# Attention and two expert layers on one core: v's row sums and a weight-conversion step placed on GpSimd

## The chip, the cores and the metric

The kernel runs on one core of a Trainium2 chip. The core has five engines with instruction streams of their own: TensorE (PE in the profile, with its weight loads as PEld), VectorE (DVE), ScalarE (ACT), GpSimd (POOL) and SyncE (SP), which here only issues DMAs. Each engine runs its stream in order and waits on semaphores for the others. The metric is the device time of one execution in microseconds, the median of the runs that were timed; lower is better.

## The reference

Inputs are q, k and v (4 batches, 8 heads, 576 positions, 64 features), and two pairs of weights, `w_in` 512 x 2048 and `w_out` 2048 x 512, all drawn as 64-bit floats. What has to be computed, cut to its core:

```python
q_d = q.reshape(B, H, Sd, 4, D).mean(axis=3)     # the same for k_d, v_d; Sd = 144
out_d = softmax(q_d @ k_d.T / 8) @ v_d           # whole rows
out_up = np.repeat(out_d, 4, axis=2)
mask = np.abs(pos[:, None] - pos[None, :]) < 4
out_local = softmax(where(mask, q @ k.T / 8, -1e9)) @ v
x = (out_up + out_local)  ->  2304 tokens x 512
h = x @ w1_in;   g = h * sigmoid(1.702 * h);  y = g @ w1_out
h = y @ w2_in;   g = elu(h);                  out = g @ w2_out
```

`mean` of four rows of v is the sum that this change is about; the kernel adds four rows and puts the factor 0.25 on the result of the product.

## The kernel before

The attention is done in units. A unit is one pair of heads of one batch: four `early` units (batch 0, windows 0 to 3) and four `late` units (batch 0, windows 4 to 8, which take the downsampled part from their early unit), then twelve units of `rest` (batches 1 to 3). `whole` is the list early + rest, the sixteen units that have a downsampled part. The two layers follow, each as products in float32r with a high and a low part of both operands: `products_h1` (L766) and `products_y1` (L801) for layer 1, `products_h2` (L914) and `products_o2` (L963) for layer 2. The first two token blocks of layer 1 (256 tokens each) run while the attention of batches 1 to 3 is still going on, and while the weights are still being converted.

**Weights.** A weight tile (128 x 512 numbers of 64 bits, `wst`) is loaded as integers and turned into a high and a low float32r part by `conv_w`. L158 takes the high words of the 64-bit numbers, read at every second word, times 2^-112 and writes `ww`; three buffers of `ww` exist. L165 (DVE) shifts in place, L168 (ACT, first 20 tiles of layer 1; for the others DVE) sets the sign bits in place, L171 (DVE) joins `ww` and the low words, L178 (ACT) makes the high part `whl`, L182 (DVE) the low part. There are 32 tiles in layer 1 (`i0, i1, o0, o1, i2, ...`; i is w_in, o is w_out) and 32 in layer 2. L158 is on ScalarE for both layers. L136 and L141 load the tiles from SP's queue.

**Rows of v.** For the product `pvd` (L582) a unit needs `vd`, where each row is the sum of four rows of v. The early units do this with `add_vd`: one load per head (`vr`, L389, from SP), and three additions on POOL (L394, L396). All units of `rest` do it with `load_vd`: row 0 by a load from SP (L378), rows 1 to 3 by DMAs from POOL's queue that add into the destination (L380), six per unit. `pv_down` of a unit starts this for the unit four places later in `whole`; `vd` has four buffers.

**Room.** Early units 1 to 3 have no room of their own for most tiles; `LENT` and `spare` give them parts of the buffers of layer-1 weights that are loaded late (o15, i15, o14, ... down to o8), and the next one, i8, holds `ones`, the operand of the filler products `keep_busy` (L853), which keep TensorE occupied at the start.

**Order.** In the start phase the code order fixes PE's stream, with two fillers after each piece of attention; elsewhere a scheduler orders the instructions of each engine by its own estimates of durations. No engine's order follows from the code alone, so the change moves instructions also on engines that it doesn't name.

Of the kernel before, what the change touches and what calls it, by code (L numbers as in the profile page):

```python
# [8 lines left out]
F32 = mybir.dt.float32  # L9
# [6 lines left out]
AF = mybir.ActivationFunctionType  # L16
ALU = mybir.AluOpType
# [3 lines left out]
D = 64  # L21
S = 576
SD = 144
HALF = 72
# [11 lines left out]
FIRST = 4  # L36

LENT = {
    "rawq": (0, "rawq", 0), "pd": (0, "pd", 0),
    "rawk": (1, "rawk", 0), "pdT": (1, "pdT", 0),  # L40
# [26 lines left out]
def kernel(  # L67
# [20 lines left out]
    nc = tc.nc  # L88
    B, H = q.shape[0], q.shape[1]
    NHP = H // 2  # L90
# [16 lines left out]
    for half in range(2):  # L107
        rows = slice(64 * half, 64 * half + 64)
        for a, e, lo in ((0, 1, -3), (1, 5, 0), (5, 6, 3)):
            m = mask[rows, a:e, :]  # L110
            for step, base, mult in ((1, -lo, -1), (-1, lo + 6, 1)):
                nc.gpsimd.affine_select(
                    out=m, in_=m, pattern=[[0, e - a], [step, KW]], compare_op=ALU.is_ge, fill=NEG,
# [30 lines left out]
    def conv_w(pool, bufs, layer, kind, f, sign):  # L144
# [8 lines left out]
        low, high = words[:, :, 0], words[:, :, 1]  # L153
        halves = t.bitcast(U16).rearrange("p (n four) -> p n four", four=4)
        w = pool.tile([P, NK * P], F32, tag="ww", name=f"ww{layer}{kind}{f}", bufs=bufs)
        wi = w.bitcast(I32)
        w3 = w.rearrange("p (c n) -> p c n", c=NK)
        nc.scalar.activation(out=w, in_=high.bitcast(F32), func=AF.Copy, scale=2.0 ** -112)  # L158

        def middle():  # L160
            shifts = [(0, 1, ALU.logical_shift_right, 13)]
# [145 lines left out]
    class Unit:  # L307
# [38 lines left out]
        def load_qk(self):  # L346
# [14 lines left out]
            for nm, src in (("q", q), ("k", k)):  # L361
# [5 lines left out]
                        out=r[:, :, j, :], in_=src[b, 2 * hp + j].rearrange("(p t) d -> p t d", t=6)  # L367
                    )
                self.raw.append(r)
        def load_vd(self):  # L370

            b, hp = self.b, self.hp
            self.vd = self.t([HALF, 2, 2, D], "vd", bufs=4)
            for r in range(4):
                for j in range(2):
                    src = v[b, 2 * hp + j].rearrange("(c g r) d -> g c r d", g=HALF, r=4)[:, :, r, :]
                    if r == 0:
                        nc.sync.dma_start(out=self.vd[:, :, j, :], in_=src)  # L378
                    else:
                        nc.gpsimd.dma_start(out=self.vd[:, :, j, :], in_=src, accum_op=ALU.add)  # L380

        def add_vd(self):

            b, hp = self.b, self.hp
            self.vd = self.t([HALF, 2, 2, D], "vd", bufs=4)
            for j in range(2):
                tag = ("gh", "gl", "gh", "g")[self.hp] if j == 0 else ("gh", "gl", "gl", "g")[self.hp]
                r = gpool.tile([HALF, 2, 4, D], F32, tag=tag, name=f"vr{j}_{self.n}", bufs=2 if tag == "g" else None)
                nc.sync.dma_start(  # L389
                    out=r.rearrange("g c r d -> g c (r d)"),  # L390
                    in_=v[b, 2 * hp + j].rearrange("(c g r) d -> g c (r d)", g=HALF, r=4),
                )
                vd = self.vd[:, :, j, :]
                nc.gpsimd.tensor_tensor(out=vd, in0=r[:, :, 0, :], in1=r[:, :, 1, :], op=ALU.add)  # L394
                for i in (2, 3):
                    nc.gpsimd.tensor_tensor(out=vd, in0=vd, in1=r[:, :, i, :], op=ALU.add)  # L396
# [181 lines left out]
        def pv_down(self):  # L578
            ps = self.ps([P, SD], "pvd")
            for kc in range(2):  # L580
                for j in range(2):
                    nc.tensor.matmul(  # L582
                        out=ps[64 * j:64 * j + 64, :], lhsT=self.vd[:, kc, j, :],
                        rhs=self.pdT[:, 2 * j + kc, :], start=(kc == 0), stop=(kc == 1),
                    )
            self.dn = self.t([P, SD], "dn", bufs=NHP)
            nc.scalar.activation(out=self.dn, in_=ps, func=AF.Copy, scale=0.25)
            at = whole.index(self) + 4
            if at < len(whole):
                whole[at].load_vd()  # L590

        def pv(self, w0, w1):
            dn = self.dn if self.dn_from is None else self.dn_from.dn
# [82 lines left out]
    whole = early + rest  # L676

    spare = [(kd, f) for f in range(NF - 1, 0, -1) for kd in "oi"]
    for part in (3, 4, 0, 1, 2):
        for u in early[1:]:  # L680
            u.lent[part] = spare.pop(0)
    following = dict(zip(units, units[1:]))
# [422 lines left out]
```

## Time and profile before

| what | value |
|---|---|
| median of 3 timed runs | 988.99 us (988.82 to 990.99) |
| span of the profiled execution | 1196.4 us, 15208 instructions |
| PE busy | 1183.7 us, 99% of the span |
| DVE, ACT, POOL busy | 503.3, 471.7, 102.0 us |
| granted TensorE clock, mean of the span | 0.750 |

The profiled execution is known by its span alone, and that is 207 us longer than the median of the timed runs. Shares and waits hold for the profiled execution; the timed ones had to be quicker somewhere. A granted clock of 1 is 2.4 GHz, a half is 1.2 GHz. Busy times are unions of an engine's instructions in a stretch, and a PE that is called busy is a model of its ends.

### The profile page before, as it was taken

What the parts mean: (1) busy time and instruction counts of PE and PEld (TensorE: products, weight loads), DVE (VectorE), ACT (ScalarE), POOL (GpSimd) and SP (SyncE); (2) the same over time, 40 slices, a digit from 0 to 9 for tenths busy, and PEclk for the clock granted to TensorE, in tenths of its full rate; (3) what the DMA queues carried; (4) which work ended last, traced back from release to release, by engine and by line L of the source; (5) the groups of instructions that cost most, each with busy time, mean ns of one, the idle gap of its engine ahead of it and who ended that gap; (6) DMA issues with size and microseconds to landing.
All of it is one profiled execution on the core that took longest, in us unless ns stands there. A gap on an engine that the chain in (4) does not pass through costs nothing.

```text
span 1196.4 us, 15208 instructions
## 1 busy us (share of the span) xinstructions
PE 1183.7 (99%) x6028; PEld 881.7 (74%) x6028; DVE 503.3 (42%) x898; ACT 471.7 (39%) x1116; POOL 102.0 (9%) x117
## 2 busy tenths in 40 slices
PE   9999999999999999999999999999999999999998
PEld 4578999976667677777668986677767777676787
DVE  3777785344453442122122796673213222221222
ACT  5888654233332441122113464553223222322233
POOL 4243210211230000000000000000000000000000
PEclk8777777776777777777777777777777777777777
DMA  9668612332331102100004940001001000100000
GB/s 194 157 157 225 145 27 39 68 58 34 47 52 23 43 16 74 44 3 33 1 1 128 315 156 0 1 14 58 1 1 35 27 1 1 44 0 1 1 36 18
DMA packets 128822, 68.04 MB, mean 57 GB/s; under 512 B 99184, under 2 KB 118768, under 8 KB 128752
## 3 DMA queue, kind: packets, MB, share of 16 engines
q1 hardware_dynamic: 109040, 63.21, 18.9%
q0 software_dynamic: 14976, 2.69, 2.7%
q10 hardware_dynamic: 4736, 1.18, 0.6%
q8 instruction: 47, 0.77, 0.3%
q14 instruction: 23, 0.19, 0.1%
HBM read 57.59 MB, written 9.44 MB: 56 GB/s over the span
## 4 chain that ended last, share of the span: by engine, by line
PE 97%; ACT 2%; DVE 1%; issue 0%; DVEq 0%; ACTq 0%
PE h L766 22%; PE y L801 21%; PE o L963 21%; PE h L914 20%; PE busy L853 3%; PE qk L468 2%; PE pv L598 2%; PE ptr L572 2%; PE qkd L495 1%; PE pvd L582 1%; PE pdt L560 1%; PE pt L421 1%; ACT pd L525 0%; DVE wst1i L165 0%; ACT sl L518 0%
## 5 line engine op out<-in xcount | busy, mean ns | idle before, releaser
L801 PE MATMUL y<-g1h,whl1o 128*128 128x256 f32 (+1 forms) x768 | 253.3, 401 | 0.0
L963 PE MATMUL o<-whl2o,g2h 128*128 128x512 f32 x576 | 214.1, 457 | 0.0
L766 PE MATMUL h<-xh,whl1i 128*128 128x256 f32 (+1 forms) x768 | 209.6, 406 | 0.3 <-ACT xh L299 0.3
L914 PE MATMUL h<-x2h,whl2i 128*128 128x512 f32 (+1 forms) x640 | 190.9, 427 | 0.0
L801 PEld LDWEIGHTS y<-g1h,whl1o 128*128 128x128 f32 x768 | 154.6, 217 | 35.6 <-issue 3.4
L766 PEld LDWEIGHTS h<-xh,whl1i 128*128 128x128 f32 x768 | 143.1, 219 | 35.2 <-issue 3.0
L924 DVE SCALAR_TENSOR_TENSOR g<-e,h 128x512 f32<-128x512 f32 (+1 forms) x80 | 50.7, 634 | 262.8 <-ACT e L922 262.6
L914 PEld LDWEIGHTS h<-x2h,whl2i 128*128 128x128 f32 x640 | 122.9, 201 | 45.6
L801 PE MATMUL y<-g1l,whl1o 128*128 128x256 f32 (+1 forms) x384 | 152.5, 397 | 0.0
L963 PEld LDWEIGHTS o<-whl2o,g2h 128*128 128x128 f32 x576 | 113.7, 199 | 46.5
L921 ACT ACTIVATE e<-h 128x512 f32<-128x512 f32 (+1 forms) x80 | 44.5, 556 | 252.2 <-PE h L914 252.2
L963 PE MATMUL o<-whl2o,g2l 128*128 128x512 f32 x288 | 131.7, 457 | 0.0
L776 ACT ACTIVATE g<-h 128x512 f32<-128x512 f32 x72 | 42.8, 596 | 202.2 <-PE h L766 200.6
L779 DVE SCALAR_TENSOR_TENSOR g<-g,h 128x512 f32<-128x512 f32 x72 | 49.1, 685 | 174.4 <-ACT g L776 174.4
L766 PE MATMUL h<-xl,whl1i 128*128 128x256 f32 (+1 forms) x384 | 107.5, 403 | 0.0
L380 POOL DMA_DIRECT2D vd<-in_v_dram x72 | 84.7, 1238 | 243.0 <-DMA vd<-in_v_dram 181.0
L914 PE MATMUL h<-x2l,whl2i 128*128 128x512 f32 (+1 forms) x320 | 95.7, 427 | 0.0
L801 PEld LDWEIGHTS y<-g1l,whl1o 128*128 128x128 f32 x384 | 83.8, 218 | 15.1 <-issue 0.3
L766 PEld LDWEIGHTS h<-xl,whl1i 128*128 128x128 f32 x384 | 72.9, 224 | 15.4 <-issue 2.0
L914 PEld LDWEIGHTS h<-x2l,whl2i 128*128 128x128 f32 x320 | 61.1, 201 | 21.7
L963 PEld LDWEIGHTS o<-whl2o,g2l 128*128 128x128 f32 x288 | 57.6, 200 | 23.9
L931 DVE TENSOR_TENSOR g2l<-g,g2h 128x512 fp32r<-128x512 f32 (+1 forms) x80 | 51.6, 645 | 36.7 <-ACT g2h L929 36.2
(110 smaller groups left out, 1185.6 us busy)
## 6 DMA issues: line engine op xcount, KB each, us to landing
wst1i<-in_moe_w_in_dram SPq DMA_DIRECT2D x16, 512.0 KB
wst1o<-in_moe_w_out_dram SPq DMA_DIRECT2D x16, 512.0 KB
wst2i<-in_moe_w_in_dram SPq DMA_DIRECT2D x16, 512.0 KB
wst2o<-in_moe_w_out_dram SPq DMA_DIRECT2D x16, 512.0 KB
ydram<-ye SPq DMA_DIRECT2D x18, 256.0 KB
out_dram<-ot SPq DMA_DIRECT2D x18, 256.0 KB
y<-ydram SPq DMA_DIRECT2D x16, 256.0 KB
vw<-in_v_dram SPq DMA_DIRECT2D x24, 122.5 KB
```

What stands on the lines that cost most here:

```text
L380: nc.gpsimd.dma_start(out=self.vd[:, :, j, :], in_=src, accum_op=ALU.add)
L468: nc.tensor.matmul(out=ps[r, w - a, :], lhsT=self.qkT[0][r, 64 * w:64 * w + 64], rhs=self.qkT[1][r, ks:ks + KW], start=not by_pe, stop=Tru ...
L766: nc.tensor.matmul(out=ph[:, i, :], lhsT=w_in(1, f, c, wp), rhs=xp[:, c, :], start=(n == 0), stop=(n == 3 * NK - 1),)
L776: nc.scalar.activation(out=g, in_=ph, func=AF.Tanh, scale=0.851)
L779: nc.vector.scalar_tensor_tensor(out=g, in0=g, scalar=1.0, in1=ph, op0=ALU.add, op1=ALU.mult)
L801: nc.tensor.matmul(out=yps[blk][m // nf][:, m % nf, :], lhsT=w_out(1, f, wp)[:, m, :], rhs=gp[:, i, :], start=(st == 0 and n == 0 and m % ...
L853: ins = nc.tensor.matmul(out=busy.rearrange("p a b -> p (a b)")[:, :n], lhsT=ones[:, :P], rhs=ones[:, :n], start=True, stop=True)
L914: nc.tensor.matmul(out=ph[:, :n], lhsT=w_in(2, f, c, wp), rhs=xp[:, c, :n], start=(i == 0), stop=(i == 3 * NK - 1),)
L921: nc.scalar.activation(out=e[:, :n], in_=ph[:, :n], func=AF.Relu, scale=-1.0)
L924: urgent["dve"] = nc.vector.scalar_tensor_tensor(out=g[:, :n], in0=e[:, :n], scalar=-1.0, in1=ph[:, :n], op0=ALU.add, op1=ALU.max)
L931: return lambda: nc.vector.tensor_tensor(out=gl[:, :n], in0=g[:, :n], in1=gh[:, :n].bitcast(F32), op=ALU.subtract)
L963: nc.tensor.matmul(out=ops[bi][i], lhsT=gp[:, i * P:(i + 1) * P], rhs=wo[wp], start=(f == 0 and m == 0), stop=(f == NF - 1 and m == 2),)
```

## The change

Three things. `load_vd` is gone; all units use `add_vd`, so that `vr` comes with one load per head and POOL adds. Outside the early units `vr` has a single buffer of its own (tag `vr` in the pool `att`), and `pv_down` starts the additions two units ahead, with two buffers of `vd` in place of four. In layer 1, the first step of `conv_w` is a `tensor_scalar` on GpSimd in place of the activation on ScalarE; layer 2 stays as it was. The `vd` of early units 1 to 3 gets a lent buffer too (part 5), so three more weight buffers are lent: i8, o7 and i7; `ones` moves to o6.

```diff
 LENT = {
-    "rawq": (0, "rawq", 0), "pd": (0, "pd", 0),
+    "rawq": (0, "rawq", 0), "vd": (5, "vd", 0), "pd": (0, "pd", 0),
...
-        nc.scalar.activation(out=w, in_=high.bitcast(F32), func=AF.Copy, scale=2.0 ** -112)
+        if layer == 1:
+            nc.gpsimd.tensor_scalar(
+                out=w, in0=high.bitcast(F32), scalar1=2.0 ** -112, scalar2=None, op0=ALU.mult
+            )
+        else:
+            nc.scalar.activation(out=w, in_=high.bitcast(F32), func=AF.Copy, scale=2.0 ** -112)
...
-        def load_vd(self):
-            self.vd = self.t([HALF, 2, 2, D], "vd", bufs=4)
-            for r in range(4):
-                for j in range(2):
...
-                    if r == 0:
-                        nc.sync.dma_start(out=self.vd[:, :, j, :], in_=src)
-                    else:
-                        nc.gpsimd.dma_start(out=self.vd[:, :, j, :], in_=src, accum_op=ALU.add)
...
         def add_vd(self):
-            self.vd = self.t([HALF, 2, 2, D], "vd", bufs=4)
+            self.vd = self.t([HALF, 2, 2, D], "vd", bufs=2)
             for j in range(2):
...
+                if self in early:
+                    r = gpool.tile([HALF, 2, 4, D], F32, tag=tag, name=f"vr{j}_{self.n}", bufs=2 if tag == "g" else None)
+                else:
+                    r = att.tile([HALF, 2, 4, D], F32, tag="vr", name=f"vr{j}_{self.n}")
...
-            at = whole.index(self) + 4
-            if at < len(whole):
-                whole[at].load_vd()
+            at = whole.index(self) + 2
+            if NHP <= at < len(whole):
+                whole[at].add_vd()
...
-    for part in (3, 4, 0, 1, 2):
+    for part in (3, 4, 0, 1, 2, 5):
```

ACT's stream at the first weight tile, before (names carry the unit or tile: `pdT_0_0_0` is early unit 0, `ww1i0` is tile i0 of layer 1):

```order
L425 ACTIVATE kd_0_2_0_398<-pt11_0_2_0_409 128x3x96
L158 ACTIVATE ww1i0_820<-wst1i0_175 128x512
L168 ACTIVATE wst1i0_175<-wst1i0_175 128x512
L565 ACTIVATE pdT_0_0_0_417<-pdt0_0_0_0_418 72x288
L178 ACTIVATE whl1i0_829<-ww1i0_820 128x512
```

and after, where the lines behind L155 have numbers that are up to five higher or four lower (L168 is L173, L565 is L561, L178 is L183):

```order
L421 ACTIVATE kd_0_2_0_398<-pt11_0_2_0_409 128x3x96
L173 ACTIVATE wst1i0_175<-wst1i0_175 128x512
L561 ACTIVATE pdT_0_0_0_417<-pdt0_0_0_0_418 72x288
L183 ACTIVATE whl1i0_815<-ww1i0_806 128x512
L514 ACTIVATE qs_0_1_0_311,sumset_110<-qk0_0_1_0_427,nm_0_1_0_426 128x70
```

The activation of `ww` has left the stream, and `pdT`, which PE waits for, stands one place nearer; so it is at 32 places.

POOL's stream after the early units' additions, before (`vd_1_0_0` is the first unit of `rest`):

```order
L396 TENSOR_TENSOR vd_0_3_0_211<-vd_0_3_0_211,vr1_0_3_0_217 72x2x64 x2
L380 DMA vd_1_0_0_491<-in_v_dram 72x2x64 x2
L380 DMA vd_1_1_0_620<-in_v_dram 72x2x64 x2
L380 DMA vd_1_2_0_716<-in_v_dram 72x2x64
L380 DMA vd_1_0_0_491<-in_v_dram 72x2x64 x2
```

and after, from tile i5 to tile i7:

```order
L159 TENSOR_SCALAR ww1i5_1116<-wst1i5_246 128x512
L390 TENSOR_TENSOR vd_1_0_0_698<-vr0_1_0_0_699 72x2x64
L392 TENSOR_TENSOR vd_1_0_0_698<-vd_1_0_0_698,vr0_1_0_0_699 72x2x64 x2
L159 TENSOR_SCALAR ww1o4_1126<-wst1o4_813 128x512
L159 TENSOR_SCALAR ww1o5_1150<-wst1o5_822 128x512
L390 TENSOR_TENSOR vd_1_0_0_698<-vr1_1_0_0_704 72x2x64
L392 TENSOR_TENSOR vd_1_0_0_698<-vd_1_0_0_698,vr1_1_0_0_704 72x2x64 x2
L159 TENSOR_SCALAR ww1i6_1197<-wst1i6_856 128x512
L390 TENSOR_TENSOR vd_1_1_0_780<-vr0_1_1_0_781 72x2x64
L392 TENSOR_TENSOR vd_1_1_0_780<-vd_1_1_0_780,vr0_1_1_0_781 72x2x64 x2
L159 TENSOR_SCALAR ww1i7_1267<-wst1i7_917 128x512
```

Seventy-two DMA issues have left POOL; 32 steps on weights and 72 additions stand there, mixed, in one stream.

SP's queue at the same place, before (`vw_0_1_4` is the window of v of late unit 1):

```order
L378 DMA vd_1_0_0_491<-in_v_dram 72x2x64 x2
L378 DMA vd_1_1_0_620<-in_v_dram 72x2x64 x2
L378 DMA vd_1_2_0_716<-in_v_dram 72x2x64 x2
L141 DMA wst1o4_827<-in_moe_w_out_dram 128x512
L378 DMA vd_1_3_0_796<-in_v_dram 72x2x64 x2
L141 DMA wst1o5_836<-in_moe_w_out_dram 128x512
L136 DMA wst1i6_870<-in_moe_w_in_dram 128x4x128
L136 DMA wst1i7_931<-in_moe_w_in_dram 128x4x128
L406 DMA vw_0_1_4_948<-in_v_dram 70x4x64
```

and after:

```order
L385 DMA vr0_1_0_0_699<-in_v_dram 72x2x256
L141 DMA wst1o4_813<-in_moe_w_out_dram 128x512
L141 DMA wst1o5_822<-in_moe_w_out_dram 128x512
L385 DMA vr1_1_0_0_704<-in_v_dram 72x2x256
L136 DMA wst1i6_856<-in_moe_w_in_dram 128x4x128
L136 DMA wst1i7_917<-in_moe_w_in_dram 128x4x128
L385 DMA vr0_1_1_0_781<-in_v_dram 72x2x256
L141 DMA wst1o6_977<-in_moe_w_out_dram 128x512
L141 DMA wst1o7_987<-in_moe_w_out_dram 128x512
L385 DMA vr1_1_1_0_786<-in_v_dram 72x2x256
L402 DMA vw_0_1_4_934<-in_v_dram 70x4x64
```

The loads of `vd` that stood ahead of weights o4 to i7 are gone; four loads of `vr`, which share one buffer, stand between weights and ahead of late unit 1's `vw`.

## Rows read from the trace of the kernel before

**Rows 1.** The page: busy us (share) xinstructions by engine; granted clock in 40 slices.
```profile
PE 1183.7 (99%) x6028; PEld 881.7 (74%) x6028; DVE 503.3 (42%) x898; ACT 471.7 (39%) x1116; POOL 102.0 (9%) x117
...
PEclk8777777776777777777777777777777777777777
```

**Rows 2.** The page, the chain that ended last, share of the span by line.
```profile
PE h L766 22%; PE y L801 21%; PE o L963 21%; PE h L914 20%; PE busy L853 3%; PE qk L468 2%; PE pv L598 2%; PE ptr L572 2%; PE qkd L495 1%; PE pvd L582 1%; PE pdt L560 1%; PE pt L421 1%; ACT pd L525 0%; DVE wst1i L165 0%; ACT sl L518 0%
```

**Rows 3.** Busy time of each engine by stretch of the span; the columns are in the first row.
```profile
core 0: us, PE busy (x) PEld busy (x) DVE busy (x) ACT busy (x) POOL busy (x), PEclk, DMA share, GB/s
15.00:130.00 115.00, 111.17 (x882) 80.76 (x881) 85.08 (x176) 95.63 (x266) 40.25 (x42) 0.75 0.75 191
130.00:210.00 80.00, 80.00 (x639) 75.42 (x637) 59.45 (x112) 41.89 (x115) 16.16 (x14) 0.75 0.27 47
210.00:420.00 210.00, 206.21 (x1283) 151.65 (x1283) 90.62 (x180) 74.11 (x263) 38.36 (x35) 0.74 0.27 47
420.00:1197.00 777.00, 772.78 (x3178) 566.71 (x3176) 266.17 (x428) 255.68 (x466) 0.00 (x0) 0.75 0.12 39
```

**Rows 4.** PE's waits in 15 to 130 us: line, releaser, us in total, times, longest.
```profile
PE pdt L560 <- DVE pd L548: 2.1, 2, 1.1
PE pdt L560 <- ACT ww1i L158: 0.8, 1, 0.8
```

**Rows 5.** ACT's busy time on L158 alone, by stretch.
```profile
15.00:130.00 115.00, 13.33 (x20) 0.75 0.75 191
130.00:210.00 80.00, 8.04 (x12) 0.75 0.27 47
```

**Rows 6.** Timeline at the first weight tile: start us, us, engine, line (ACT, then PE).
```profile
24.45 0.66 ACT L158 ACTIVATE ww1i<-wst1i 128x512 f32<-128x512 f32 x1
25.00 1.36 ACT L168 ACTIVATE wst1i<-wst1i 128x512 f16<-128x512 f32 x1
...
25.24 0.48 PE L560 MATMUL pdt<-ident,pd 72*72 72x72 f32 x4 [0.82 <-ACT ww1i L158]
```

**Rows 7.** DVE's timeline while POOL adds rows of v (first two) and after it (third).
```profile
26.40 0.98 DVE L171 SCALAR_TENSOR_TENSOR ww1i<-ww1i,wst1i 128x512 int32<-128x512 int32 x1 [0.28 <-ACT wst1i L168]
...
28.18 0.87 DVE L182 TENSOR_TENSOR whl1i<-ww1i,whl1i 128x512 fp32r<-128x512 f32 x1
...
33.03 0.69 DVE L182 TENSOR_TENSOR whl1i<-ww1i,whl1i 128x512 fp32r<-128x512 f32 x1
```

**Rows 8.** POOL's operations by line: ns min/median/max, first and last start, form.
```profile
L394 POOL TENSOR_TENSOR vd<-vr x8: 449/454/897, 9.6 to 30.8; 72x128 f32<-72x128 f32 x8
...
L112 POOL TENSOR_SCALAR_AFFINE_SELECT mask<-mask x12: 237/249/451, 1.6 to 4.7; 64x70 bf16<-64x70 bf16 x8, 64x280 bf16<-64x280 bf16 x4
```

**Rows 9.** DVE's busy time on L171, then on L182, 15 to 130 us.
```profile
15.00:130.00 115.00, 14.10 (x20) 0.75 0.75 191
...
15.00:130.00 115.00, 12.45 (x18) 0.75 0.75 191
```

**Rows 10.** The page: POOL's DMA issues with the idle time ahead of them.
```profile
L380 POOL DMA_DIRECT2D vd<-in_v_dram x72 | 84.7, 1238 | 243.0 <-DMA vd<-in_v_dram 181.0
```

**Rows 11.** SP's longest waits for vd, and its timeline around weights o5 to i7.
```profile
SPq L378 <- PE pvd L582: 100.5, 10, 20.2
...
69.42 0.74 SPq L378 DMA_DIRECT2D vd<-in_v_dram  x2
...
70.62 0.98 SPq L136 DMA_DIRECT2D wst1i<-in_moe_w_in_dram  x2
78.35 1.73 SPq L406 DMA_DIRECT2D vw<-in_v_dram  x4
```

**Rows 12.** The last filler in the chain of waits; PE where late unit 1 first uses vw.
```profile
70.76 0.63 PE busy L853 x2
...
84.45 0.98 PE L598 MATMUL pv<-PT,vw 70*64 70x64 f32 x20
```

**Rows 13.** DVE makes the tenth w_in low part; PE's products in which it is first read.
```profile
126.67 0.68 DVE L182 TENSOR_TENSOR whl1i<-ww1i,whl1i 128x512 fp32r<-128x512 f32 x1
...
126.56 1.47 PE L766 MATMUL h<-xh,whl1i 128*128 128x256 f32 x8
```

More of the change, by code (lines that the diff above doesn't have):

```diff
@@ L369, in load_qk @@
                 self.raw.append(r)
-        def load_vd(self):
-            b, hp = self.b, self.hp
-            self.vd = self.t([HALF, 2, 2, D], "vd", bufs=4)
-            for r in range(4):
-                for j in range(2):
-                    src = v[b, 2 * hp + j].rearrange("(c g r) d -> g c r d", g=HALF, r=4)[:, :, r, :]
-                    if r == 0:
-                        nc.sync.dma_start(out=self.vd[:, :, j, :], in_=src)
-                    else:
-                        nc.gpsimd.dma_start(out=self.vd[:, :, j, :], in_=src, accum_op=ALU.add)
         def add_vd(self):
             b, hp = self.b, self.hp
-            self.vd = self.t([HALF, 2, 2, D], "vd", bufs=4)
+            self.vd = self.t([HALF, 2, 2, D], "vd", bufs=2)
             for j in range(2):
                 tag = ("gh", "gl", "gh", "g")[self.hp] if j == 0 else ("gh", "gl", "gl", "g")[self.hp]
-                r = gpool.tile([HALF, 2, 4, D], F32, tag=tag, name=f"vr{j}_{self.n}", bufs=2 if tag == "g" else None)
+                if self in early:
+                    r = gpool.tile([HALF, 2, 4, D], F32, tag=tag, name=f"vr{j}_{self.n}", bufs=2 if tag == "g" else None)
+                else:
+                    r = att.tile([HALF, 2, 4, D], F32, tag="vr", name=f"vr{j}_{self.n}")
                 nc.sync.dma_start(
```

## The prediction

> **What bounds the kernel now.** I read the page first. PE is busy for 1183.7 us of 1196.4, so only 12.7 us of idle PE exist in the whole profiled execution, and no edit off PE can take more than those out of it [rows 1]. The granted clock is 0.75 nearly throughout, between the two levels 1.2 and 2.4 GHz [rows 1]. The chain of waits says the same: four product lines hold 22 + 21 + 21 + 20 = 84% of the span [rows 2], that is 0.84 x 1196.4 = 1005 us. The timed runs take 988.99 us in all, less than these four lines alone. So in the timed runs PE was faster than in the profile, and the profile's own slack can't be carried over. I give the timed runs two bounds. If all of PE's work shrank with the total, the factor is 988.99 / 1196.4 = 0.827, a mean clock of 0.75 / 0.827 = 0.91. If the clock was full, the factor is 0.75, and the rest was waiting. DVE and ACT don't shrink with it.
>
> The table by stretch then shows where that matters [rows 3]. From 420 us on PE is busy 772.8 of 777 us and DVE and ACT are a third of it: nothing there. From 210 to 420 us DVE has 90.6 and ACT 74.1 us of work beside 206 on PE: nothing there at either factor. From 15 to 130 us, though, PE has 111.2 us, ACT 95.6 and DVE 85.1; times 0.827 PE has 91.9, times 0.75 it has 83.4, and ACT with 95.6 is the longest at both. From 130 to 210 us PE has 80.0 (66.2 and 60.0), DVE 59.5, ACT 41.9. The change takes work from ACT in just the stretch where ACT is the longest. How near the conversion is to its user shows in one place: the tenth w_in tile is done on DVE at 126.67 + 0.68 = 127.35 us, and the eight products from 126.56 us on turn to it after about six of them, at about 127.6 us [rows 13].
>
> **ScalarE loses L158.** Its 32 activations of layer 1 are 20 up to 130 us (13.33 us) and 12 behind (8.04 us) [rows 5]. They overlap their followers: one starts at 24.45 us and the next instruction at 25.00, so each takes 0.55 us of ACT's stream, not 0.66 [rows 6]. Removed are 20 x 0.55 = 11.0 us and 12 x 0.55 = 6.6 us. ACT goes to 84.6 us in the first stretch, and in the second to 35.3, where it was never the longest. Directly on PE's path the profile shows one such wait, 0.8 us ahead of `pdt` [rows 4, 6]; it goes for the most part.
>
> **GpSimd gains L159.** Its operation is not in the trace. Bounds by rows: the select on 70 columns takes 237 ns at least and the longest on 280 columns 451, about 1.0 ns a column, which gives 0.69 us for 512; the two-input additions on 128 columns take 0.45 us, four times which is 1.8 [rows 8]. I take 0.8, near the lower end, since L159 reads one input. In the first stretch that is 20 x 0.8 = 16 us, by the upper bound 20 x 1.8 = 36. With the additions there (18 of early units, 12 of `rest`, at 0.5 about 15 us) POOL has at most 51 of 115 us: its total is no bound. The Trainium skill ("GPSIMD Engine Reference", § 3.1) gives 769 ns for 512 elements in a tight loop; no run here shows that. By it the 32 steps would be 25 us of POOL, and the sum is as it is.
>
> **The rows of v.** 72 issues of 1.24 us leave POOL, and with them 243 us in which POOL waited ahead of them [rows 10]; nobody on PE waits for that. They become 72 additions at 0.45 us, 32 us in all, of which 12 lie before 130 us, 18 before 210 and 42 behind, where DVE has room. I cost the removal at nothing, since PE's busy time hides it.
>
> **DVE pays.** Where POOL adds rows of v in the profile, DVE's L171 took 0.98 and L182 0.87 us, against 0.69 without POOL beside it [rows 7], and POOL's own additions stretched from 0.45 to 0.90 us [rows 8]. So each meeting costs DVE 0.18 to 0.29 us, say 0.25. L171 and L182 are 14.1 + 12.5 = 26.6 us of the first stretch [rows 9]; with the other DVE operations that read two tiles from SBUF (L300, L548, L781) I estimate 40 of 115 us. The 32 new POOL operations there (20 + 12) meet one of them at its start about every second time: 16 x 0.25 = 4 us, between 0 and 32 x 0.29 = 9.3. DVE goes from 85.1 to 89.1 (85.1 to 94.4). In the second stretch 30 operations cost as much: 59.5 + 4 = 63.5 (59.5 to 68.2).
>
> **The queues.** SP no longer stops at L378 for PE's `pvd` (100.5 us in ten waits; weights i6 and i7 stood behind the one that ended at 69.42 us [rows 11]). Instead it stops at `vr`, whose one buffer comes free when POOL has added, and POOL's additions stand behind L159 steps that wait for a `ww` buffer, and so for L182. Behind SP's stop stand weights o4 to o7 and late unit 1's `vw`. That load went out at 78.35 us and took 1.73 us to issue [rows 11]; PE reads it at 84.45 [rows 12], 4.4 us after that. The order puts it behind two units' additions, which I place at about 80 us; I charge 0.5 us, between 0 and 2. The lent buffers (i8, o7, i7) come free with early units 1 to 3, the last with the `pvd` for which SP waited until 69.42 us anyway [rows 11], and `ones` (now o6) with the last filler at 71.4 us [rows 12], ahead of which o6 was not loaded before either (its load follows `vw` at 78.35): nothing.
>
> **The sum.** At factor 0.827 the longest engine of the first stretch goes from ACT's 95.6 to PE's 91.9: -3.7. The second stays with PE at 66.2. With the queue +0.5: -3.2. At factor 0.75 the first goes from 95.6 to DVE's 89.1: -6.5; the second from 60.0 to 63.5: +3.5; with +0.5: -2.5. The place seen in the profile adds -0.8 to either. That is -4.0 and -3.3; against the profile's own 1196.4 us it is no more than -0.8 + 0.5, about nothing, since PE is there the longest anyway. I forecast -4.0: 985.0 us.
>
> **Rivals.** (a) *The whole relief arrives.* If ACT in its order, not only its total, holds PE, then 11.0 us go, and with the second stretch's part up to 12: 977 to 980 us. For it: ACT leads in the stretch, and a stream with waits in it is worse than its total. Against it: DVE is 10.5 us behind ACT and most of PE's charged waits are DVE's, 2.1 of the three us [rows 4].
> (b) *Nothing to measure.* The timed runs wait as little there as the profile does, and their lower time has its source elsewhere: -1.5 to +1.5, 987.5 to 990.5 us. For it: 3.8 us of idle PE in the first stretch [rows 3]. Against it: ACT's 95.6 us can't shrink.
> (c) *DVE becomes the bound, slower.* A POOL operation on weights is longer than an addition, and a DVE operation that meets it stands until it ends. At 0.8 us the mean rest is 0.4 us. If each operation is met, the first stretch costs 20 x 0.4 + 12 x 0.25 = 11 us, DVE 96.1 against ACT's 95.6: +0.5; the second 12 x 0.4 + 18 x 0.25 = 9.3, DVE 68.8 against PE's 66.2: +2.6. With the queue's 2 us that is +5, 994 us. It decides from 10.5 us of added DVE time on. For it: rows 7 show the meeting; against it: they show 0.29 at most. The Trainium skill ("SBUF — State Buffer", "Who interferes with whom") speaks against this change: a DVE operation with two SBUF inputs and a GpSimd operation that reads SBUF exclude each other for a whole instruction. The profile's stretched operations on both sides agree with it [rows 7, 8]; for L159 no run here shows it.
> (d) *The step doesn't leave the path.* L159 at 1.8 us behind additions that wait for `vr` reaches L171 later than L158 did; with the tenth tile used as it is made [rows 13], each lateness goes to PE. With two of the 1.0 us that L159 would be longer than taken, twice over the queue's 2: +2 to +4, 991 to 993.
>
> **How the numbers follow.** Forecast (-2.5 to -6) 0.44; (a) 0.16; (b) 0.22; (c) and (d) 0.18 together. The range leaves out half of (a)'s far end and half of (c): 978 to 992 us. A measurement of this kernel can tell about 0.2%, 2.0 us. Faster by more than that: forecast and (a), 0.60; within: (b), 0.22; slower: (c) and (d), 0.18.
>
> **What would show it.** In the profile after: ACT's busy time from 15 to 130 us about 11 to 13 us lower; L159 at 0.7 to 1.8 us; L171 and L182 over 0.69 us in about half of their instances, and DVE 3 to 9 us fuller; SP's waits for `pvd` replaced by waits for POOL; a span within 2 us of 1196 if the clock is again 0.75. Wrong would be: ACT's relief there, the timed runs unchanged (then the stretch was PE's in them, too); or PE waiting for `whl` or `vw`, which it does nowhere now.

## The result, and the profile after

The changed kernel takes 1000.87 us (median of four timed runs, 999.72 to 1001.2) against 989.99 us for the kernel before on the same chip (988.82 to 992.52). The ratio is 1.0108 with a 95% interval of 1.0084 to 1.0131: about 11 us slower. The forecast was 985.0 us, in a range of 978 to 992. (One execution of the last kernel below took 1871 us where its nine others took 986 to 991; it is left out.)

The front's profile of the kernel before ran at a clock of 0.75, and its rows can't be set against a profile at 0.98. The kernel before was therefore profiled again (first experiment below): span 990.5 us at a mean clock of 0.983. All comparisons below are with that execution. First busy time by engine on the page, of before (990.5 us) and of after (997.9 us, clock 0.979); they answer to [rows 1].

```profile
PE 957.3 (97%) x6028; PEld 789.2 (80%) x6028; DVE 497.9 (50%) x898; ACT 468.5 (47%) x1116; POOL 102.4 (10%) x117
```

```profile
PE 962.4 (96%) x6028; PEld 793.2 (79%) x6028; DVE 506.9 (51%) x898; ACT 453.9 (45%) x1084; POOL 123.6 (12%) x149
```

ACT has lost 14.6 us, DVE has gained 9.0 and POOL 21.2. The table by stretch, before and then after, answers to [rows 3]; the columns are in its first row.

```profile
core 0: us, PE busy (x) PEld busy (x) DVE busy (x) ACT busy (x) POOL busy (x), PEclk, DMA share, GB/s
15.00:130.00 115.00, 102.45 (x984) 77.91 (x985) 92.35 (x195) 101.96 (x286) 40.45 (x45) 0.93 0.82 200
130.00:210.00 80.00, 77.90 (x836) 73.70 (x835) 63.98 (x126) 48.54 (x151) 25.28 (x20) 1.00 0.40 65
```

```profile
15.00:130.00 115.00, 98.93 (x892) 74.18 (x889) 92.17 (x186) 87.98 (x255) 65.31 (x52) 0.88 0.67 193
130.00:210.00 80.00, 76.33 (x782) 72.15 (x779) 67.49 (x123) 40.66 (x128) 30.41 (x29) 0.98 0.29 61
```

ScalarE is relieved by 14 us in the first stretch (it runs 31 instructions fewer there; 24 of them are L158, the others come later), and TensorE does less there, not more: 892 matmuls in place of 984, at a clock of 0.88 in place of 0.93. A landmark shows that all is decided early. The first `ye` (the result of layer 1 for the first token block) starts at 191.9 us before and at 201.7 after; from there to the end of the span it is 798.6 and 796.2 us.

PE's waits of `pdt` for DVE, before and after (us in total, times, longest), answer to [rows 4], but for the whole span. The softmax operands `pd` and `sl` come later than before:

```profile
PE pdt L560 <- DVE pd L548: 2.2, 3, 1.1
...
PE pdt L560 <- DVE sl L483: 1.3, 2, 0.8
```

```profile
PE pdt L556 <- DVE pd L544: 6.3, 3, 2.8
...
PE pdt L556 <- DVE sl L479: 3.4, 1, 3.4
```

They aren't the price by themselves: the kernel with v's part alone, which costs nothing (below), has 4.6 us in the `pd` row.

GpSimd's step itself, in the groups of instructions (count | busy us, mean ns | idle time ahead and what ended it):

```profile
L159 POOL TENSOR_SCALAR ww1i<-wst1i 128x512 f32<-128x512 f32 x16 | 33.8, 2115 | 31.5 <-DVE nmd L499 9.1 <-DVE whl1i L187 8.2 <-DMA wst1i<-in_moe_w_in_dram 5.9
L159 POOL TENSOR_SCALAR ww1o<-wst1o 128x512 f32<-128x512 f32 x16 | 31.1, 1952 | 24.8 <-DVE whl1i L187 10.9 <-ACT whl1i L183 8.3 <-DVE whl1o L187 2.9
```

It takes 2.0 us on average, where 0.8 was taken. By single instructions (min/median/max, in ns) it is 1.51 us at least:

```profile
L159 POOL TENSOR_SCALAR ww1i<-wst1i x16: 1513/1805/5365, 20.7 to 158.8; 128x512 f32<-128x512 f32 x16
```

### The profile page after: what moved, and what is told of

The parts are those of the page before. It is cut to its first block, busy times and chain, and to the rows that moved or that the text cites. A ratio compares the mean times of both kernels' runs of the same rounds, so it can differ in the third digit from the quotient of the medians.

```text
span 997.9 us, 15234 instructions
## 1 busy us (share of the span) xinstructions
PE 962.4 (96%) x6028; PEld 793.2 (79%) x6028; DVE 506.9 (51%) x898; ACT 453.9 (45%) x1084; POOL 123.6 (12%) x149
## 5 line engine op out<-in xcount | busy, mean ns | idle before, releaser
L797 PE MATMUL y<-g1h,whl1o 128*128 128x256 f32 (+1 forms) x768 | 208.0, 344 | 0.0
L959 PE MATMUL o<-whl2o,g2h 128*128 128x512 f32 x576 | 181.1, 394 | 2.8 <-ACT ye L806 2.5
L762 PE MATMUL h<-xh,whl1i 128*128 128x256 f32 (+1 forms) x768 | 170.8, 347 | 4.0 <-ACT xh L304 2.9
L910 PE MATMUL h<-x2h,whl2i 128*128 128x512 f32 (+1 forms) x640 | 159.0, 370 | 0.0
L797 PEld LDWEIGHTS y<-g1h,whl1o 128*128 128x128 f32 x768 | 135.2, 191 | 17.0 <-issue 1.0
L762 PEld LDWEIGHTS h<-xh,whl1i 128*128 128x128 f32 x768 | 124.9, 192 | 22.2 <-ACT xh L304 3.6
L910 PEld LDWEIGHTS h<-x2h,whl2i 128*128 128x128 f32 x640 | 114.5, 188 | 22.6
L797 PE MATMUL y<-g1l,whl1o 128*128 128x256 f32 (+1 forms) x384 | 130.3, 340 | 0.0
L959 PE MATMUL o<-whl2o,g2l 128*128 128x512 f32 x288 | 113.2, 393 | 0.0
L762 PE MATMUL h<-xl,whl1i 128*128 128x256 f32 (+1 forms) x384 | 88.3, 346 | 0.0
L925 ACT ACTIVATE g2h<-g 128x512 fp32r<-128x512 f32 (+1 forms) x80 | 47.1, 589 | 42.8 <-DVE g L920 42.7
L776 ACT ACTIVATE g1h<-g 128x512 fp32r<-128x512 f32 x72 | 45.5, 631 | 46.4 <-DVE g L775 46.3
```

Source lines behind the costliest of these rows:

```text
L762: nc.tensor.matmul(out=ph[:, i, :], lhsT=w_in(1, f, c, wp), rhs=xp[:, c, :], start=(n == 0), stop=(n == 3 * NK - 1),)
L776: ins = nc.scalar.activation(out=gh, in_=g, func=AF.Copy)
L797: nc.tensor.matmul(out=yps[blk][m // nf][:, m % nf, :], lhsT=w_out(1, f, wp)[:, m, :], rhs=gp[:, i, :], start=(st == 0 and n == 0 and m % ...
L910: nc.tensor.matmul(out=ph[:, :n], lhsT=w_in(2, f, c, wp), rhs=xp[:, c, :n], start=(i == 0), stop=(i == 3 * NK - 1),)
L925: nc.scalar.activation(out=gh[:, :n], in_=g[:, :n], func=AF.Copy)
L959: nc.tensor.matmul(out=ops[bi][i], lhsT=gp[:, i * P:(i + 1) * P], rhs=wo[wp], start=(f == 0 and m == 0), stop=(f == NF - 1 and m == 2),)
```

## The experiments

All times are medians; a ratio is to the kernel before, run beside it on the same chip, with its 95% interval.

**The kernel before, once more.** No edit, for a second profile.

> The kernel before, unchanged, for a second profile of it. If the granted clock is near 1 in this execution, the span should be about 987 us (the timed median less some 2 us, as 1000.9 against 997.9 after the change), and PE should then show waits in the first 200 us that the first profile (clock 0.75) hid. Contention theory: DVE busy about 85 us from 15 to 130 us and not full from 130 to 170 us, where after the change it is busy 40.0 of 40 us. Queue theory: POOL and SP waits reach PE in neither.

One run of 992.31 us, span 990.5 at clock 0.983: the rows above. DVE has 92.35 us in the first stretch, not 85, and it is busy for 39.9 of the 40 us from 130 to 170, as it is after the change (39.99). A VectorE that the change alone fills, which contention had as its sign, is not there.

**The two halves of the change, and the step left out.** v's part alone takes back the step:

```diff
-        if layer == 1:
-            nc.gpsimd.tensor_scalar(
...
-        else:
-            nc.scalar.activation(out=w, in_=high.bitcast(F32), func=AF.Copy, scale=2.0 ** -112)
+        nc.scalar.activation(out=w, in_=high.bitcast(F32), func=AF.Copy, scale=2.0 ** -112)
```

> Only the part on v's rows (one load per head, additions on GpSimd, the buffers and the lending as in the change); the weight step stays on ScalarE. Contention theory: additions of 0.45 us meet DVE little, so -2 to +2 us against before. Queue theory (vr's single buffer holds SP, and POOL's additions hold each other up): +4 to +11 us. Order theory (the scheduler's new order costs, whichever part is made): anything up to +11.

990.51 us, ratio 1.0002 (0.9984 to 1.002). v's part costs and gains nothing. The other half keeps the step and has `load_vd` with its adding DMAs back, as in the diff of the front:

> Only the weight step of layer 1 on GpSimd; v's rows come by adding DMAs as before, whose issues then stand in one POOL stream with the weight steps. Contention theory (32 operations of 1.5 to 1.8 us that exclude DVE's two-input operations): +7 to +11 us, with DVE's L171/L182 counterparts over 1 us where POOL is beside them. Queue theory: the weight steps behind adding DMAs that wait for PE's pvd come late, which shows as DVE waiting for POOL, also slower, +5 or more; if POOL's steps are on time and it is slower, it was DVE.

1026.46 us, ratio 1.036 (1.0307 to 1.0412). The timelines of POOL, DVE and PE (start us, duration, ..., idle time before it and its releaser) show why in one chain:

```profile
56.46 3.75 POOL L159 TENSOR_SCALAR ww1i<-wst1i 128x512 f32<-128x512 f32 x2 [3.29 <-DVE whl1i L187]
60.15 2.47 POOL L385 DMA_DIRECT2D vd<-in_v_dram  x2
...
94.79 1.15 POOL L385 DMA_DIRECT2D vd<-in_v_dram  x1 [0.74 <-issue]
95.53 1.98 POOL L159 TENSOR_SCALAR ww1o<-wst1o 128x512 f32<-128x512 f32 x1
...
97.54 0.69 DVE L176 SCALAR_TENSOR_TENSOR ww1o<-ww1o,wst1o 128x512 int32<-128x512 int32 x1 [21.22 <-POOL ww1o L159]
...
106.22 0.45 PE L464 MATMUL qk<-mask,identb 128*128 128x350 bf16 x1 [26.19 <-DVE PT L579]
```

From 60 to 95 us POOL issues eighteen adding DMAs of later units, over 1.1 us each and with pauses, and no step stands among them. The next tile's step begins behind them, DVE stands 21.2 us for it, and PE 26.2 us for DVE. In this stream two kinds of work stand in one order, and the one that waits holds up the other. With v's adds as POOL instructions this stall is gone, so the two parts of the change belong together.

Next the step is left out of the kernel before altogether (VectorE joins the unscaled high words, so the weights are other numbers): ScalarE's relief at no price.

```diff
-        nc.scalar.activation(out=w, in_=high.bitcast(F32), func=AF.Copy, scale=2.0 ** -112)
+        if layer == 2:
+            nc.scalar.activation(out=w, in_=high.bitcast(F32), func=AF.Copy, scale=2.0 ** -112)
...
-                out=wi, in0=wi, scalar=3, in1=low, ...
+                out=wi, in0=high if layer == 1 else wi, scalar=0 if layer == 1 else 3, in1=low, ...
```

> The weight step of layer 1 is left out altogether: DVE joins the high words themselves (read at every second word) with the low words, so layer 1's weights are other numbers. ScalarE is relieved of the same 32 operations, and GpSimd gets nothing. It is the most that the relief of ScalarE can be worth. Contention theory: -3 to -8 us (the relief is real, the price on GpSimd and DVE ate it). Rival (ScalarE isn't the bound, as DVE is): -1 to +1 us.

991.38 us, ratio 1.0003 (0.998 to 1.0027). Its table has ACT at 90.32 us in the first stretch where before has 101.96, and PE gains nothing from it:

```profile
15.00:130.00 115.00, 103.94 (x973) 78.50 (x972) 92.20 (x195) 90.32 (x261) 43.23 (x44) 0.90 0.78 198
```

So the gain that was forecast does not exist, whoever does the step.

**The same in the changed kernel, a memset in the step's place, and half the tiles.** The edit of the third kernel in the changed one, then `nc.gpsimd.memset(w, 2.0 ** -112)` in place of L159, then the step on GpSimd for the first and for the last 16 tiles alone:

```diff
-        if layer == 1:
+        begun.append(f)
+        if layer == 1 and len(begun) <= 16:        # > 16 in the fourth
```

> The changed kernel with the exponent step of layer 1 left out altogether (VectorE joins the unscaled high words, so the weights are other numbers): v's part is kept, neither ScalarE nor GpSimd does the step. v's part alone measured 990.5 us and the step left out alone 991.4, so if the price sits in GpSimd's step, by whatever way, this gives 988 to 993 us. If it is the meeting of the two parts in the program's order (v's new loads and the relieved ScalarE), it stays at 997 us or more.

990.51 us, ratio 1.0014 (0.9993 to 1.0034).

> The changed kernel with GpSimd's read-and-multiply of layer 1 replaced by a memset of the same tile to 2^-112 (the weights are other numbers): same place in GpSimd's stream, same dependences, nothing read from SBUF. Theory X, GpSimd's reading holds up VectorE's copies: VectorE's rows beside it go back to those of the kernel with v's part alone (0.76 us for the uint16 shift), time 989 to 993 us. Theory L, the length and place of GpSimd's step in the chain of a tile's conversion: the time falls only by the share by which the memset is shorter than 1.5 us; at 0.5 us about 993 to 995 us, at 1 us or more 996 to 1000 us.

990.36 us, ratio 1.0002 (0.9986 to 1.0018). The memset takes 0.52 us at the median. It has the step's place in the stream, but it is shorter, reads nothing, and so doesn't wait for the load of its tile either; this run parts none of the three.

> The changed kernel with the step of the first 16 tiles of layer 1 on GpSimd and that of the last 16 on ScalarE. In the profile of the changed kernel the first lag stands already at the last filler (70.0 us against 63.2 with v's part alone) and grows to 10.4 us by 202 us. If the price arises in the start stretch, where the first tiles are converted beside the attention: 997 to 1001 us. If it arises from 130 to 170 us, where VectorE is full and the later tiles are converted: 990 to 994 us. A price in proportion to the tiles gives 995 to 996 us.

995.77 us, ratio 1.0057 (1.0036 to 1.0077).

> The changed kernel with the step of the first 16 tiles of layer 1 on ScalarE and that of the last 16 on GpSimd, the counterpart of the run before. Price in the start stretch: 989 to 993 us. Price in the stretch from 130 to 170 us: 997 to 1001 us. In proportion: 995 to 996 us. If the two halves together make more than the whole price, the two stretches do not add.

994.89 us, ratio 1.0046 (1.003 to 1.0062). The price is spread over the tiles, and the two halves add up to the whole. No single place in the start phase makes it.

**Length against read, the dose, and VectorE's load.** Three memsets in place of the step; the step reading `ident`, four times over; the step twice; and, in the kernel with v's part alone, VectorE's join L171 left out in layer 1 (other weights).

```diff
+            nc.gpsimd.memset(w, 2.0 ** -112)       # x3, in place of L159
...
-                out=w, in0=high.bitcast(F32), scalar1=2.0 ** -112, ...
+                out=w3, in0=ident[:, None, :].to_broadcast([P, NK, P]), scalar1=2.0 ** -112, ...
```

> The changed kernel with GpSimd's read-and-multiply of layer 1 replaced by three memsets of the same tile, one after the other (the weights are other numbers): 3 x 0.55 us where it is alone is 1.65 us, about as long as the step's 1.5, with the same dependences, but nothing is read. The single memset cost nothing (990.4 us) and is both shorter and without a read; this run parts the two. If the price is the length of GpSimd's step in the chain of a tile's conversion: 998 to 1002 us, as the changed kernel. If it is what the read does to VectorE: 989 to 993 us.

995.14 us, ratio 1.0042 (1.0024 to 1.006): between the two expectations. Length without a read makes nearly half of the price.

> The changed kernel with GpSimd's multiply of layer 1 kept, but reading the 128x128 identity four times over, in neighbouring 4-byte words, in place of the staged weights' high words, which lie 8 bytes apart (the weights are other numbers). If the 1.5 us of the step come from the spaced read, this takes 0.7 to 1.0 us alone; if from the element count, 1.4 to 1.6 us. The time should follow the length: near 990 to 994 us in the first case, 998 to 1002 in the second. If VectorE's rows stay stretched at the short length, the read itself is what disturbs it.

1000.37 us, ratio 1.0095 (1.0068 to 1.0123). The multiply of neighbouring words takes 1.48 us at least, as the one of spaced words takes 1.51:

```profile
L159 POOL TENSOR_SCALAR ww1i<-ident x16: 1482/1571/5292, 14.3 to 157.4; 128x512 f32<-128x512 f32 x16
```

So its length doesn't come from the spacing of the words. Nor does the wait for the tile's load matter, which this multiply hasn't. In these two kernels and in the one with a single memset, the streams of PE, DVE, ACT and SP hold the same instructions in the same order as in the changed kernel; only POOL's differ. From 990.4 to 1000.9 us, then, the difference is POOL's alone, and no other engine's order has a part in it. The three memsets and the multiply of `ident` also keep POOL equally busy, as the first rows of their pages show, and yet the multiply costs 5.2 us more:

```profile
PE 958.5 (97%) x6028; PEld 790.2 (80%) x6028; DVE 505.7 (51%) x898; ACT 453.3 (46%) x1084; POOL 116.9 (12%) x213
```

```profile
PE 963.7 (96%) x6028; PEld 794.0 (79%) x6028; DVE 503.3 (50%) x898; ACT 452.6 (45%) x1084; POOL 117.0 (12%) x149
```

So the rest of the price needs the read, in some way.

> The changed kernel with GpSimd's step of every tile of layer 1 issued twice (the same result written twice), which doubles its 65 us to some 130. If the price is in proportion to GpSimd's step, by its length or its reads, it doubles: 1009 to 1014 us. If the price is a fixed one of being in GpSimd's stream at all, it stays at 999 to 1003 us. If GpSimd becomes the longest engine of the start stretch (its 65.3 of 115 us there would be some 105), it is more than double: above 1016 us.

1018.47 us, ratio 1.0282 (1.0265 to 1.03): the second step costs 17.6 us, the first 10.4. That is more than double, though POOL's stretch stands at 92 of 115 us, below the 105 I had named.

> The kernel with v's part alone (step on ScalarE, 990.5 us) with VectorE's join of the two words left out in layer 1 (32 x 0.70 = 22.3 us of VectorE less, spread over the first 170 us; the weights are other numbers). If VectorE is the engine that sets the time up to 200 us, as the 10.0 of 10 us from 130 to 170 us in the changed kernel suggest, this is 975 to 985 us. If no single engine is the bound and the start is set by TensorE and its clock, 988 to 992 us.

987.89 us, ratio 0.9982 (0.9968 to 0.9996). DVE's page total falls from 499.1 to 482.1 us and the time by 2.6. A microsecond of VectorE is worth some 0.15 us here (0.04 to 0.21 by the scatter of the runs), so the 7.8 us of DVE that the changed kernel has over v's part alone (506.9 against 499.1) would be worth about 1.2 by this rate. That speaks against a price by VectorE's longer rows alone, and the next runs put it to the test.

**Load without waiting.** The kernel with v's part alone, and GpSimd multiplies each finished low part into a scratch tile that nothing reads. Room for it comes from two `ww` buffers in place of three, which is the control; then the unread multiply once, and twice. The streams of PE, DVE, ACT and SP are the same in the first two, row by row.

```diff
-    wt1 = Weights(1, order1, stage1, 3, lambda tag: True, NSIGN)
+    wt1 = Weights(1, order1, stage1, 2, lambda tag: True, NSIGN)
...
             wts[layer, kind, f] = hl
+            if layer == 1:
+                beside = pool.tile([P, NK * P], F32, tag="wx", name=f"wx{kind}{f}", bufs=1)
+                nc.gpsimd.tensor_scalar(out=beside, in0=hl[:, 1]..., scalar1=2.0 ** -112, ...)
```

> The control for the next two: the kernel with v's part alone (step on ScalarE, 990.5 us) with two conversion buffers ww in place of three, which makes room for a scratch tile. 990 to 995 us; a third buffer that mattered would show as more.

991.93 us, ratio 1.0021 (1.0004 to 1.0038).

> The control, and after each of the 32 tiles of layer 1 GpSimd multiplies the finished low part of the tile into a scratch tile that nothing reads: 128x512 float32 as in the step, the same load on GpSimd and SBUF, but no other engine waits for it, and the rows on TensorE, VectorE, ScalarE and SyncE stand in the same order as in the control. If the price of the change is what GpSimd's work does to the rows beside it (VectorE's above all): 6 to 12 us over the control. If it is that a tile's conversion waits for a slower engine: within 2 us of the control.

997.13 us, ratio 1.0079 (1.0056 to 1.0101): 5.2 us over the control, just below what contention had predicted.

> The same with that unread multiply issued twice for every tile. Contention: about twice the price of the single one, 12 to 25 us over the control, as the step issued twice (1018.5 us) had it. Waiting: still within 3 us of the control, unless v's adds, which stand behind the multiplies in GpSimd's stream, come too late; then GpSimd's row to TensorE's pvd would show it.

1011.59 us, ratio 1.0222 (1.0185 to 1.0259): 19.7 us over it. By these runs alone contention would be half the price. But the multiplies still stand in front of v's adds in POOL's stream. SP's wait for POOL's last add on `vd`, in the control, with one and with two multiplies (us in total, times, longest):

```profile
SPq L380 <- POOL vd L387: 36.0, 5, 16.6
```

```profile
SPq L386 <- POOL vd L393: 58.5, 10, 13.8
```

```profile
SPq L390 <- POOL vd L397: 79.6, 10, 27.9
```

With two, PE waits for a late load of v itself, which it does for 1.7 us with one and not at all in the control:

```profile
PE pv L599 <- DMA vw<-in_v_dram: 9.8, 3, 5.7
```

**The same without v on GpSimd.** v's sums are left out: one row of every four goes straight into `vd` (other numbers), so that POOL has nothing of v and SP waits for no `vr`.

```diff
-                nc.sync.dma_start(
-                    out=r.rearrange("g c r d -> g c (r d)"), ...
-                vd = self.vd[:, :, j, :]
-                nc.gpsimd.tensor_tensor(out=vd, in0=r[:, :, 0, :], in1=r[:, :, 1, :], op=ALU.add)
...
+                nc.sync.dma_start(out=self.vd[:, :, j, :], in_=v[b, 2 * hp + j].rearrange(...)[:, :, 0, :])
```

> The control for the next: the kernel with v's part alone (step on ScalarE), but v's sums left out: one row of every four goes straight from DRAM into vd, so GpSimd has nothing of v and SyncE waits for no buffer of v's rows (vd holds other numbers). 985 to 991 us: v's adds alone cost nothing so far.

990.13 us, ratio 1.0001 (0.9983 to 1.0019). The control: step on ScalarE, POOL nearly empty.

> The changed kernel with the same left out: GpSimd has the step of layer 1 and nothing of v. If part of the price is that v's adds stand behind the step in GpSimd's one stream, and SyncE's loads behind those (the wait of SyncE for vd rose from 41.9 us with v's part alone to 56.9), this falls by that part, to 993 to 997 us; if the price is contention and the wait for the step alone, it is 8 to 11 us over the control as the changed kernel is over v's part alone, 997 to 1001 us.

994.27 us, ratio 1.0049 (1.003 to 1.0068): 4.1 us over the control. The changed kernel is 10.4 us over v's part alone.

> The kernel with the unread multiply of 32 tiles on GpSimd (997.1 us, 5.2 over its control), with v's sums left out in the same way. Nothing waits for GpSimd now, neither a conversion nor v. What is left over the control without v's sums is contention alone: 5 us if the queue of v's adds was no part of the 5.2, within 2 us if it was all of it.

990.47 us, ratio 0.9997 (0.998 to 1.0014): 0.3 us over the control, within the error. (It has two `ww` buffers where the control has three, and the scheduler has ordered its streams anew; two buffers cost some 1.4 us above.) The pages of the control and of this kernel:

```profile
PE 959.9 (97%) x6028; PEld 789.9 (80%) x6028; DVE 497.3 (50%) x898; ACT 469.2 (47%) x1116; POOL 4.7 (0%) x21
```

```profile
PE 958.0 (97%) x6028; PEld 789.5 (80%) x6028; DVE 501.4 (51%) x898; ACT 469.6 (47%) x1116; POOL 82.5 (8%) x53
```

POOL has 78 us more work and DVE's rows are 4.1 us longer beside it. Contention is there, and where nothing waits for GpSimd it costs no time that can be measured.

**What the runs add up to.** Of the changed kernel's 10.4 us over v's part alone, about 4 remain when GpSimd has the step and nothing of v. Since the unread multiply costs nothing there, the likely cause is that a tile's conversion hangs on an engine that takes 1.5 us at least, and 2.3 on average in that kernel, for what ScalarE did in 0.68. The waits of DVE name it:

```profile
DVE ww1i L176 <- POOL ww1i L159: 1.9, 2, 1.4
DVE ww1o L176 <- POOL ww1o L159: 1.4, 1, 1.4
```

The other 6 us or so (4 to 8 by the scatter of the runs) come only with v's adds in the same stream; by what way is argued from here on. POOL's timeline after shows how they meet:

```profile
115.24 1.85 POOL L159 TENSOR_SCALAR ww1o<-wst1o 128x512 f32<-128x512 f32 x1 [8.30 <-ACT whl1i L183]
...
142.23 1.72 POOL L159 TENSOR_SCALAR ww1i<-wst1i 128x512 f32<-128x512 f32 x1 [2.64 <-ACT kT L421]
143.92 0.45 POOL L390 TENSOR_TENSOR vd<-vr 72x128 f32<-72x128 f32 x1
144.34 1.51 POOL L159 TENSOR_SCALAR ww1o<-wst1o 128x512 f32<-128x512 f32 x1
145.82 1.55 POOL L392 TENSOR_TENSOR vd<-vd,vr 72x128 f32<-72x128 f32 x2
```

And SP's, in the same kernel:

```profile
116.70 0.35 SPq L385 DMA_DIRECT2D vr<-in_v_dram  x1
...
147.40 0.31 SPq L385 DMA_DIRECT2D vr<-in_v_dram  x1
147.75 1.76 SPq L402 DMA_DIRECT2D vw<-in_v_dram  x4
149.61 1.24 SPq L371 DMA_DIRECT2D rawq<-in_q_dram  x2
```

The rows of v are asked for at 116.70 us. Their add is nothing slow, 0.45 us, but after that load went out POOL still does seven steps, most of which wait for DVE or ACT first, and the add runs at 143.92. SP stands for PE's `pv` until 133.14, and then for 13.4 us at the single `vr` buffer; behind it stand `vw` and the q and k of the next units. With v's part alone the same places read:

```profile
121.71 1.26 POOL L385 TENSOR_TENSOR vd<-vr 72x128 f32<-72x128 f32 x1 [48.90 <-DMA vr<-in_v_dram]
...
127.92 0.31 SPq L380 DMA_DIRECT2D vr<-in_v_dram  x1
...
130.13 1.24 SPq L366 DMA_DIRECT2D rawq<-in_q_dram  x2
```

There POOL has waited for the rows, not the rows for POOL; the add runs 22.2 us earlier and the next q 19.5 us earlier. But the queue at this place is not the whole of that. An add also needs the `vd` buffer that `pvd` of the unit two places ahead reads, and this product (first row of each pair) is 11.1 us later already. The pairs are of v's part alone, of the changed kernel, and of the kernel with the step and nothing of v; the second row is the next unit's `pvd`:

```profile
118.46 0.71 PE L573 MATMUL pvd<-pdT,vd 72*64 72x144 f32 x8
146.59 0.71 PE L573 MATMUL pvd<-pdT,vd 72*64 72x144 f32 x8
```

```profile
129.54 0.71 PE L578 MATMUL pvd<-pdT,vd 72*64 72x144 f32 x8
160.64 0.71 PE L578 MATMUL pvd<-pdT,vd 72*64 72x144 f32 x8
```

```profile
121.22 0.71 PE L569 MATMUL pvd<-pdT,vd 72*64 72x144 f32 x8
152.44 0.71 PE L569 MATMUL pvd<-pdT,vd 72*64 72x144 f32 x8
```

From one to the next PE takes 28.1, 31.1 and 31.2 us. The changed kernel loses 3 us here, and the kernel without any add in the queue loses as much. The rows show an add that stands behind the steps; they don't show that the 6 us are lost there.

**What stays open.** By what way the 10 us come is argued, not shown. SP's wait for POOL's adds, the sign of the queue, doesn't follow the price: it is 53.5 us with one memset (no price), 57.0 with three (nearly half of it) and 56.9 after.

```profile
SPq L383 <- POOL vd L390: 53.5, 9, 12.2
```

```profile
SPq L385 <- POOL vd L392: 57.0, 10, 12.3
```

```profile
SPq L385 <- POOL vd L392: 56.9, 9, 13.4
```

The two ways of halving the price, without a read and without v's adds, were not tried together. A read that costs only where something waits for GpSimd is not excluded. Leaving out v's adds removes the queue, but also 62 us of POOL's own work (67.0 against 4.7 on the pages) and three quarters of the bytes of the `vr` loads, and lets the scheduler order the other streams anew. The kernel with one memset has its add at 135.12 us, 13 us later than v's part alone, at no price; so there is slack in that queue. Where it is used up, no row shows. A second `vr` buffer, for which the stage has no room beside the conversion buffers, wasn't tried. None of the versions that compute the reference beats the kernel before.

## Why the prediction was wrong

**The factor for the timed runs** (its first part) was the first failed step. It scaled PE's 111.2 us of the first stretch to 83 to 92 us and so made ACT, with 95.6, the longest engine. At a clock of 0.93 the new profile has PE busy for 102.45 us in that stretch, ACT for 101.96. It isn't the same work (984 matmuls, where [rows 3] have 882), but beside each us of ACT PE now has 1.00, where it had 1.16: a factor of 0.86, above both bounds. ACT and PE are level, and ACT was not ahead by 4 to 12 us.

**"The longest engine sets the stretch"** failed with it. Leaving out 11.6 us of ACT gave nothing (1.0003), and leaving out 17 us of DVE gave 2.6 us. Engines that wait for each other in turn don't act like a row of bars of which the tallest counts. Rival (b) had this half right.

**L158's removal** was sized rightly: 11.6 us of ACT in the first stretch of the kernel without the step, where 11.0 were counted and 11 to 13 named as the sign. It had no value, and that is the forecast's -3.7 to -6.5 us, and the -0.8 of PE's one wait with it.

**L159** was mis-sized: 0.8 us was taken, near the lower bound, because it reads one input. It measured 1.51 us at the least and 2.0 on average, above the upper bound of 1.8, which came from the additions. The Trainium skill ("GPSIMD Engine Reference", § 3.1) has 769 ns for 512 elements in a tight loop, as the best case; this instruction took 1.48 us at the least for either spacing, and that decides here.

**v's rows at nothing** held: 1.0002. **The lent buffers** at nothing held, too, since they are part of that kernel.

**DVE pays 4 us** a stretch: the size was fair (9.0 us on the page in all), the price was not, as far as it is DVE's longer rows alone. The unread multiply showed it at 0.3 us, within the error. So rival (c), on the right side with 994 us, isn't borne out as it stands: DVE is as full before as after from 130 to 170 us. That the three memsets cost about half of what the multiply does keeps some part for the read. The Trainium skill ("SBUF — State Buffer", "Who interferes with whom") has a two-input DVE operation and a GpSimd operation that reads SBUF contend. The trace agrees that rows stretch: L176 has 0.69 us at the median and 1.53 at most. It also has the shift L170, with one input, at up to 1.34 us beside a median of 0.75 in layer 2. Whether anyone waits for a longer row is another matter, and beside the unread multiply hardly anyone did.

**The queue at 0.5 us, between 0 and 2**, was too small by several us, if the 6 us that come only with v's adds are the queue's; that is argued, not shown. The prediction did name it: additions behind steps that wait for a `ww` buffer, and `vw` behind SP's stop. It judged by one place (`vw` at about 80 us, 4.4 us of slack); from 117 to 147 us stands a longer stop, 13.4 us of SP, beside which PE loses 3.

The sum had no term for **the step on the path** at all; it was left to a rival. It measured about 4 us without v's adds. **Rival (d)**, the step on the path and the queue, at 991 to 993 us, comes nearest: 4 us for the step where it had 2, and 6 with v's adds where it had up to 2. Its chance shared 0.18 with (c).

## What to carry to other kernels

Before you move work onto an idle engine, write down its stream in order and ask of every other job in it who waits for that, and what the new work itself waits for: an engine with 10% busy time is not free if the new job stands there waiting in front of an old one. An engine's share in a stretch says what it could lose, not what it is worth; leave the work out once, and the run tells what its removal can bring at best. And a load test must not share a queue with anything that is waited for: here contention looked like half the price until v's adds were out of the stream.

## What the runs showed of the hardware

TensorE's clock takes part in the loss. In slices of 10 us up to the first `ye`, PE's idle time and the time that its work lost to a clock below 1 (busy time times one minus the clock) come to 19.0 + 4.2 us with v's part alone, 22.6 + 12.8 in the changed kernel and 32.5 + 19.1 with the step twice. The first `ye` starts at 187.8, 201.7 and 218.3 us; less the two terms that is 164.6, 166.3 and 166.7. So in these executions, one of each kernel, the lost clock is more than half of what separates the first two. But kernels without a price lose nearly as much by the clock: before it is 19.7 + 7.8 us, and in the control without v's sums 16.4 + 10.6. The idle time, 16.4 to 19.7 us in these three and 22.6 after, tells the price better. In one place the clock falls right after idle time: in the changed kernel PE is idle for 4.0 us from 40 to 50 us, for want of `xh` and `pd`, and the clock granted from 50 to 60 us is 0.63, so that a filler (L849, two matmuls) takes 0.95 us where it took 0.55 at 42 us. There 4.0 us of waiting were followed by 3.7 us of work lost to the clock.

A multiply of 128 x 512 float32 on GpSimd took 1.48 to 1.51 us at the least, with words 4 or 8 bytes apart, and a memset of the same tile 0.52. Beside VectorE's work single multiplies took up to 6.2 us.
